# A fused attention and two-layer kernel: earlier weight stores, attention tile by tile, operands built in the last products

## The chip, the cores and the metric

The kernel runs on one core of a Trainium2 chip. The metric is the device time of one execution in microseconds, taken as the median of the runs shown. The core's engines work side by side, each through its own instructions in order: TensorE (PE in the profile, with PEld for its weight loads), VectorE (DVE), ScalarE (ACT), GpSimd (POOL) and SyncE (SP), which in this kernel issues every DMA.

## The reference, cut to what matters

```python
out[c] = softmax(scale * q_c @ [mem_k, k_ctx].T) @ [mem_v, v_ctx]      # chunks of 32 with local context
x  = heads of out side by side                                        # 3072 tokens x 512
x  = (sigmoid(x @ w_gate) * (x @ w_val)) @ w_out                       # 512 -> 1536 -> 512
h  = x @ w_in                                                         # 512 -> 2048
g  = (a0 + a1 h + a2 h^2 + a3 h^3) / (1 + |b0||h| + |b1| h^2 + 1e-6)
y  = g @ w_out                                                        # 2048 -> 512
```

All inputs and the result are float32. Each operand of a large product is split into a high and a low half (fp32r), and each product is three matmuls (high by high, high by low, low by high).

## The kernel before, in words

The 3072 tokens are 24 attention tiles of 128, and 6 blocks of 512. Attention of tiles 0 to 3 comes first (to about 31 us). Then 24 steps, numbered si, run the first layer on blocks 0 and 1 directly: step si is the slice f = si mod 12 of the 1536 hidden columns for block j = si // 12. A step is a gate product (`gate_val` with m = 0, 12 matmuls at L280), its sigmoid on ACT (L289), a value product (12 more at L280), the scaling on DVE (L292), the split of the result (`g_split`, L303 on ACT and L304 on DVE) and the out product of the step before (`out1`, L315).

A dictionary `plan`, filled by `at(si, function, arguments)`, says what else each step does. Within a step the order is written out: first the DMAs (loads of queries, keys, values, raw weights, and stores), then `w1_hi` (ACT, L263: high halves of the next step's three weights), `attn_exp` (ACT, L145), `bits1` (DVE, L236 and L243: the raw weights' bits), `s_add` (POOL, L367), then the gate product, `w1_lo` (DVE, L267: low halves), `attn_sum`, `attn_mul` (DVE), the attention products (L165 and L180), `s_split` (ACT L373, DVE L374), then the value product, and last `attn_qk` and `attn_max`. ACT changes its function table between exponential and sigmoid, which is an ACT_TABLE_LOAD each way.

Attention of tiles 4 to 15 lies in these steps. Tiles 8 to 15 are done in pairs: both tiles' exponentials stand in one step (12, 14, 16, 18). A tile at a sequence's edge (t mod 6 is 0 or 5) is copied by ACT (L117) and masked by a POOL memset (L119 or L122), and DVE takes its maximum behind that (L130); the others are read from PSUM (L137, L139).

The remaining blocks use seven products of halves in place of eight (`unit_s`, L436), for s = 1 and 2. Their weights need the raw gate and value weights in DRAM (`store_raw`, L351, tensor wsd) and four sums of them for each pair of slices: `s_add(p)` makes the sums on POOL from the raw weights of slices 2p and 2p+1, `s_split(p)` splits them into X and queues their store. The out weights go to DRAM too (L352, tensor wod). Their token operands come from xd: `load_b` loads four tiles (L383), and `build` makes differences (DVE L394) and splits them into X (ACT L390, DVE L391). X holds 14 slices; `SST` lists those for the sums' splits, `XS` those for the operands. At the end of step 23 the kernel issues `load_b(1)`, the first weights (`load_a`) and `build(1)`, ahead of the last two out products.

All big tiles come from one pool of 32 buffers (`wpool`): raw weights, split weights, queries, keys, values, sums and loaded operands. A tile taken from it waits for whatever last used that buffer, a store's landing among it. Work tiles of 2 KB a partition come from `tpool` (11), PSUM has four buffers `ps`, and a gate product's buffer comes free with its sigmoid. SP issues in order, and a DMA waits there for the landing of the DMA eight places before it.

The second layer runs from about 723 us. Its weights' splits are placed by `weights2`.

Of the kernel before, what the change touches and what calls it, by code (L numbers as in the profile page):

```python
# [8 lines left out]
F32 = mybir.dt.float32  # L9
# [12 lines left out]
P = 128  # L22
# [19 lines left out]
def fused_kernel(ctx: ExitStack, tc: tile.TileContext, q, k, v, w1, w2, coef, x2d, w2d, xd, gd, wsd, wod, out):  # L42
# [21 lines left out]
    cab = const.tile([P, 2], F32, name="cab")  # L64
    qc = const.tile([P, 1], F32, name="qc")
    nc.gpsimd.memset(qc, QC)

# [128 lines left out]
    def flush():  # L198
        for out_, in_ in pending:
            nc.sync.dma_start(out=out_, in_=in_)  # L200
        pending.clear()
# [137 lines left out]

    IDX = dict(A11=0, S2=1, S1=2, S3=3, A12=4, S4=5, A22=6)  # L340
    XS = (0, 2, 8, 10, 12, 4, 6)
    SST = (0, 1, 2, 3)

    def store_raw(f):

        p, odd = divmod(f, 2)
        for m in range(2):
            w = wp[1, 1, f, m].rearrange("p b (h k) -> p b h k", h=2)
            for name, h in ((("A22", 1),) if odd else (("A11", 0), ("A12", 1))):
                dst = wsd[p, :, m, IDX[name]].rearrange("p (b k) -> p b k", b=2)  # L350
                nc.sync.dma_start(out=dst, in_=w[:, :, h].bitcast(F32))  # L351
        nc.sync.dma_start(out=wod[f], in_=wp[1, 1, f, 2].bitcast(F32))  # L352

    ssum = {}
# [14 lines left out]

    def s_split(p):  # L370
        for i, (n, t) in enumerate(ssum.pop(p).items()):
            u = X[:, SST[i]].rearrange("p m (b k) -> p m b k", b=2)
            nc.scalar.activation(out=u[:, :, 0], in_=t, func=ACTF.Copy)  # L373
            nc.vector.tensor_tensor(out=u[:, :, 1], in0=t, in1=u[:, :, 0].bitcast(F32), op=ALU.subtract)  # L374
            pending.append((wsd[p, :, :, IDX[n]], X[:, SST[i]].bitcast(F32)))

    braw = {}

# [6 lines left out]
    def build(s):  # L385


        def split(i, t):
            hi, lo = (X[:, XS[i] : XS[i] + 2, b] for b in range(2))
            nc.scalar.activation(out=hi, in_=t, func=ACTF.Copy)  # L390
            nc.vector.tensor_tensor(out=lo, in0=t, in1=hi.bitcast(F32), op=ALU.subtract)  # L391

        def sub(out_, a, b):
            nc.vector.tensor_tensor(out=out_, in0=a, in1=b, op=ALU.subtract)  # L394

        b11, b12, b21, b22 = braw[0, 0], braw[0, 1], braw[1, 0], braw[1, 1]
        braw.clear()
        u1, u2 = (wpool.tile([P, 2, 512], F32, tag="w", name=f"bt{s}_{i}") for i in range(2))
        sub(u1, b12, b11)
        split(0, b11)  # L400
        sub(u2, b22, u1)
        split(1, u2)
        split(2, u1)
        sub(b12, b22, b12)
        split(3, b12)
        sub(u2, b21, u2)

        return [lambda: split(4, b21), lambda: split(5, b22), lambda: split(6, u2)]

    ast, wo = {}, {}  # L410

# [221 lines left out]
    def at(si, *call):  # L633
        plan.setdefault(si, []).append(call)
# [10 lines left out]
            if f > 2:  # L645
                at(max(si - 3, 0), load_w1, f)

    for t in range(4, 16, 2):
        s0 = (2, 5, 10, 12, 14, 16)[t // 2 - 2]
        for o, u in ((0, t), (1, t + 1)):  # L650
            at(s0 + o - 2, load_qk, u)
            at(s0 + o, attn_qk, u)
            at(s0 + o, attn_max, u)
            if t < 8:
                at(s0 + 3, attn_exp, u)
                at(s0 + o + 3, load_v, u)
                at(s0 + o + 3, attn_sum, u)
                at(s0 + o + 3, attn_mul, u)
                at(s0 + o + 4, attn_t, u)
                at(s0 + o + 5, pv, u)  # L660
            else:
                at(s0 + 2, attn_exp, u)
                at(s0 + o + 1, load_v, u)
                at(s0 + 2, attn_sum, u)
                at(s0 + 2, attn_mul, u)
                at(s0 + 3, attn_t, u)
                at(s0 + 4, attn_raw, u)

    for p, si in enumerate((11, 13, 15, 16, 18, 20)):
        at(si, s_add, p)  # L670
        at(si + 1, s_split, p)
    for f in range(NF1):
        at(NF1 + f, store_raw, f)
    w2_next = 0

    def weights2(k, n):
# [53 lines left out]
    with tc.manual_schedule():  # L730
# [69 lines left out]
        for si, (j, f, c0, n) in enumerate(steps):  # L800
            acts = plan.get(si, [])

            def run(*fns):
                for fn, *args in acts:
                    if fn in fns:
                        fn(*args)

            flush()
            run(load_qk, load_v, load_w1, store_raw)
            run(w1_hi, attn_exp, bits1, s_add)  # L810
            gate_val(j, f, 0, c0, n)
            run(w1_lo, attn_sum, attn_mul, pv, attn_raw, attn_t, s_split)
            gate_val(j, f, 1, c0, n)
            run(scale1)
            g_split((1, j, f, c0), sgs.pop((j, f, c0)), n)
            run(attn_qk, attn_max)
            if si == len(steps) - 1:
                flush()
                load_b(1)
                load_a(1, 0, 0)  # L820
                load_a(1, 0, 1)
                rest = build(1)
            if si:
                out1(*steps[si - 1])
        out1(*steps[-1])
        n_point = 0
        for s in range(1, NB // 2):
            for p in range(NP1 + 1):
                for m in range(2):
                    if p < NP1:  # L830
                        if m == 0:
                            load_wo(s, 0, 2 * p)
                        else:
                            load_wo(s, 0, 2 * p + 1)
                        if p == NP1 - 1:
                            load_wo(s, 1, m)
                            load_g(s, m)
                        unit_s(s, p, m, rest)
                        rest = []
                        load_a(s, p + 1, m)  # L840
                        point(n_point, s, 2 * (p - 1) + m if p else -1)
                        n_point += 1
                    else:
                        flush()
                        if m == 0:
                            load_g(s, 2)
                            load_wo(s, 1, 2)
                            if s == 1:
                                load_b(2)
                        out_s(s, 0, NF1 - 2 + m)  # L850
                        if m == 0:
                            g_split((1, 2 * s + 1, 0, 0), gb.pop(0), 512)
            for f in range(NF1):
                last = s == NB // 2 - 1
                load_wo(s, 1, f + 3)
                load_g(s, f + 3)
                if f + 1 < NF1:
                    g_split((1, 2 * s + 1, f + 1, 0), gb.pop(f + 1), 512)
                if last:
                    if f == 0:  # L860
                        nc.scalar.activation(out=cab, in_=cf[:, 4:6], func=ACTF.Abs)
                    if f >= NF1 - PRE:
                        h2(0, f - NF1 + PRE)
                if not last or f < NF1 - 1:
                    out_s(s, 1, f)
                if last:
                    if f % 2 == 0 and f < 2 * KT:
                        load_x2(0, f // 2)
                    if f % 2 == 1 and f < 2 * KT:
                        split_x2(0, f // 2)  # L870
                    if f == NF1 - 1:
                        for i in range(PRE - 1):
                            recip2(0, i)
                            ratio2(0, i)
                        split2(0, 0)
                    w2_next = weights2(w2_next, 2)
                elif f == 4:
                    load_a(2, 0, 0)
                    load_a(2, 0, 1)
                    rest = build(2)  # L880
        steps2 = [(j, f) for j in range(NB) for f in range(NF2)]
        for si in range(PRE, len(steps2) + LAG2):
            if si < len(steps2):
                j, f = steps2[si]
                if j == 0:
                    w2_next = weights2(w2_next, 1 if f > PRE + 1 else 0)
                if j + 1 < NB:
                    if f % 3 == 0 and 0 < f <= 3 * KT:
                        load_x2(j + 1, f // 3 - 1)
                    if f % 3 == 2 and 3 < f < 3 * KT + 3:  # L890
                        split_x2(j + 1, f // 3 - 1)
                h2(j, f)
                if si == PRE:
                    out_s(NB // 2 - 1, 1, NF1 - 1)
            if si >= LAG2:
                out2(*steps2[si - LAG2])
            if si - 1 < len(steps2):
                recip2(*steps2[si - 1])
                ratio2(*steps2[si - 1])
            if si - 2 < len(steps2):  # L900
                split2(*steps2[si - 2])
# [75 lines left out]
```

## Time and profile before

| | us |
|---|---|
| median of 3 runs | 1261.28 (1261.0 to 1262.39) |
| the profiled execution | 1263.89 |
| its span | 1262.0 |
| PE busy | 1173.4 (93%) |
| DVE busy | 951.7 (75%) |
| ACT busy | 717.9 (57%) |
| POOL busy | 37.1 (3%) |

The span is the time from the profile's first instruction to its last; 1.9 us of the execution lie around it. PE is busy for 93% of the span, but the share is an average over parts with different limits: cut into 40 slices of 31.5 us, PE is busy for six tenths of the time from 158 to 221 us, and the DMA engines for three tenths from 95 to 158 us. The rows below show these places.

### The profile page before, as it was taken

The page shows a single profiled execution, that of the slowest core. Times are in us where ns is not written, and L with a number is a line of the kernel's source. Part 1 is how long each engine was busy: PE and PEld are TensorE (multiplying, and loading weights), DVE is VectorE, ACT ScalarE, POOL GpSimd, SP SyncE. Part 2 cuts the span into 40 slices and gives each one's busy share as a digit, 9 for nine tenths or more (in the row PEclk, how much of TensorE's full clock was granted, in tenths as well). Part 3 has the DMA queues.
Part 4 walks back from the last instruction along what each step waited for, and adds up shares of the span by engine and source line. Part 5 has one row for each costly group of instructions (what it writes and reads, how often), then busy time and mean ns, then how long its engine had stood idle before and what let it go on. Part 6 is the DMA issues. An engine that isn't in the chain of part 4 may idle for free.

```text
span 1262.0 us, 20397 instructions
## 1 busy us (share of the span) xinstructions
PE 1173.4 (93%) x7920; PEld 952.0 (75%) x7920; DVE 951.7 (75%) x1496; ACT 717.9 (57%) x1222; POOL 37.1 (3%) x39
## 2 busy tenths in 40 slices
PE   4999966998999997899999899999999999999998
PEld 3787745786777776678888678788888888888887
DVE  6887546955766664467776579999888888898886
ACT  5876245653344341243333478886676677776765
POOL 0000103400000000000000000000000000000000
PEclk8999987999999999899999999999999999999999
DMA  9763358879988866779986932010010010100000
GB/s 369 275 200 114 121 199 288 295 251 328 358 313 320 320 244 237 288 271 358 355 327 216 381 126 59 26 51 17 9 51 9 9 50 9 50 17 1 34 1 34
DMA packets 95280, 220.22 MB, mean 175 GB/s; under 512 B 9168, under 2 KB 26576, under 8 KB 95184
## 3 DMA queue, kind: packets, MB, share of 16 engines
q1 hardware_dynamic: 95184, 218.93, 48.6%
q8 instruction: 62, 1.02, 0.3%
q14 instruction: 34, 0.28, 0.1%
HBM read 159.12 MB, written 59.77 MB: 173 GB/s over the span
## 4 chain that ended last, share of the span: by engine, by line
PE 47%; DVE 5%; DMA 2%; ACT 1%; issue 1%; SPq 0%; DVEq 0%; ACTq 0%
PE acc L577 19%; PE h L538 18%; PE u L436 7%; PE acc L490 3%; DMA w2f<-w2d 2%; DVE t L565 1%; DVE X L304 1%; DVE qq L564 1%; DVE wp L267 0%; DVE qq L551 0%; DVE t L550 0%; DVE t L549 0%; DMA wo<-wod 0%; DVE c L460 0%; DMA x2d<-x2s 0%
## 5 line engine op out<-in xcount | busy, mean ns | idle before, releaser
L538 PE MATMUL h<-X,wp 128*128 128x512 f32 x1152 | 276.7, 389 | 2.4 <-DVE wp L267 2.4
L577 PE MATMUL acc<-wp,X 128*128 128x512 f32 x1152 | 276.6, 389 | 1.0 <-ACT x2s L331 1.0
L538 PEld LDWEIGHTS h<-X,wp 128*128 128x128 f32 x1152 | 216.1, 188 | 47.7 <-DVE wp L267 2.8
L577 PEld LDWEIGHTS acc<-wp,X 128*128 128x128 f32 x1152 | 216.0, 188 | 46.8 <-ACT x2s L331 1.6
L436 PE MATMUL u<-X,a 128*128 128x512 f32 x1008 | 237.7, 393 | 11.1 <-DVE X L391 3.3
L436 PEld LDWEIGHTS u<-X,a 128*128 128x128 f32 x1008 | 188.8, 189 | 56.8 <-DVE c L460 5.0
L490 PE MATMUL acc<-g,wo 128*128 128x512 f32 x576 | 146.8, 404 | 17.6 <-ACT g L303 14.0
L280 PE MATMUL h<-X,wp 128*128 128x512 f32 x576 | 147.8, 410 | 9.7 <-ACT sg L289 6.2
L546 ACT ACTIVATE t<-h,cf 128x512 f32<-128x512 f32 x96 | 74.7, 778 | 123.1 <-PE h L538 119.9
L490 PEld LDWEIGHTS acc<-g,wo 128*128 128x128 f32 x576 | 109.1, 193 | 45.5 <-ACT g L303 16.3
L280 PEld LDWEIGHTS h<-X,wp 128*128 128x128 f32 x576 | 112.4, 198 | 36.0 <-ACT sg L289 6.9
L460 DVE TENSOR_TENSOR c<-c,u 128x512 f32<-128x512 f32 x168 | 111.5, 684 | 23.5 <-PE u L436 21.0
L549 DVE TENSOR_TENSOR t<-t,h 128x512 f32<-128x512 f32 x96 | 65.8, 686 | 40.5 <-ACT hh L548 39.0
L303 ACT ACTIVATE g<-sg 128x512 fp32r<-128x512 f32 x24 | 15.2, 632 | 121.5 <-DVE sg L453 121.5
L550 DVE SCALAR_TENSOR_TENSOR t<-t,cf,h 128x512 f32<-128x512 f32 x96 | 71.8, 748 | 3.4
L564 DVE SCALAR_TENSOR_TENSOR qq<-qq,y 128x512 f32<-128x512 f32 x96 | 65.8, 686 | 9.1 <-ACT y L559 9.1
L558 ACT ACTIVATE y<-qq,qc 128x512 f32<-128x512 f32 x96 | 69.9, 728 | 3.6 <-DVE qq L551 3.2
L551 DVE SCALAR_TENSOR_TENSOR qq<-hh,cab,qq 128x512 f32<-128x512 f32 x96 | 71.7, 747 | 0.0
L565 DVE SCALAR_TENSOR_TENSOR t<-t,cf,y 128x512 f32<-128x512 f32 x96 | 71.6, 746 | 0.0
L315 PE MATMUL acc<-X,wp 128*128 128x512 f32 x288 | 71.0, 396 | 0.0
L566 DVE SCALAR_TENSOR_TENSOR t<-qq,t 128x512 f32<-128x512 f32 x96 | 66.5, 693 | 3.3
L547 ACT ACTIVATE qq<-h,cab 128x512 f32<-128x512 f32 x96 | 65.4, 681 | 3.3 <-DVE t L565 3.3
(82 smaller groups left out, 1263.6 us busy)
## 6 DMA issues: line engine op xcount, KB each, us to landing
a<-wsd SPq DMA_DIRECT2D x72, 512.0 KB, 8.9
st<-w_in SPq DMA_DIRECT2D x68, 512.0 KB, 6.4
wo<-wod SPq DMA_DIRECT2D x48, 512.0 KB, 7.2
v<-v_in SPq DMA_DIRECT2D x24, 512.0 KB, 6.8
wsd<-X SPq DMA_DIRECT2D x24, 512.0 KB, 4.4
k<-k_in SPq DMA_DIRECT2D x24, 416.0 KB, 5.5
wsd<-wp SPq DMA_DIRECT2D x36, 256.0 KB, 5.2
w2d<-c SPq DMA_DIRECT2D x32, 256.0 KB, 4.1
```

What stands on the lines that cost most here:

```text
L280: nc.tensor.matmul(pt, lhsT=w[:, a, kt * P : (kt + 1) * P], rhs=x[:, kt, b, c0 : c0 + n], start=(kt == 0 and i == 0), stop=(kt == KT - 1 a ...
L315: nc.tensor.matmul(acc[j][d][:, c0 : c0 + n], lhsT=w[:, a, d * P : (d + 1) * P], rhs=g[:, b, 0:n], start=(f == 0 and c0 == 0 and i == 0), ...
L436: nc.tensor.matmul(bank, lhsT=w[:, a * 256 + kt * P : a * 256 + kt * P + P], rhs=X[:, XS[i] + kt, b], start=(kt == 0 and n == 0), stop=(kt ...
L460: nc.vector.tensor_tensor(out=out_, in0=a, in1=b, op=ALU.add)
L490: nc.tensor.matmul(acc[j][d], lhsT=w[:, a, d * P : (d + 1) * P], rhs=g[:, b], start=(f == 0 and i == 0), stop=(f == NF1 - 1 and i == 2),)
L538: nc.tensor.matmul(hp, lhsT=w[:, a, kt * P : (kt + 1) * P], rhs=x[:, kt, b], start=(kt == 0 and i == 0), stop=(kt == KT - 1 and i == 2),)
L546: nc.scalar.activation(out=t, in_=hp, func=ACTF.Identity, scale=cf[:, 3:4], bias=cf[:, 2:3])
L550: nc.vector.scalar_tensor_tensor(out=t, in0=t, scalar=cf[:, 1:2], in1=hp, op0=ALU.add, op1=ALU.mult)
L551: nc.vector.scalar_tensor_tensor(out=qq, in0=hh, scalar=cab[:, 1:2], in1=qq, op0=ALU.mult, op1=ALU.add)
L564: nc.vector.scalar_tensor_tensor(out=qq, in0=qq, scalar=QC, in1=y, op0=ALU.add, op1=ALU.mult)
L565: nc.vector.scalar_tensor_tensor(out=t, in0=t, scalar=cf[:, 0:1], in1=y, op0=ALU.add, op1=ALU.mult)
L577: nc.tensor.matmul(acc[j][m], lhsT=g[:, a, m * P : (m + 1) * P], rhs=w[:, b], start=(f == 0 and i == 0), stop=(f == NF2 - 1 and i == 2),)
```

## The change

The raw gate and value weights go to DRAM from the split weights of block 0 (steps 0 to 11) and not of block 1 (12 to 23); the out weights' store becomes `store_out` and stays in steps 12 to 23. Tiles 8 to 15 get a step each for every part of their attention. The sums' splits go round six slices of X, not four. `load_b(1)` moves to the start of step 22, `build(1)` is cut in two and its halves stand between the products of step 23 and ahead of `out1(22)`. `load_b(2)` moves behind the first out product of its block. The second layer calls `weights2` in two more of its steps, so its splits run two calls earlier. A tile of 32 bytes a partition stands before X.

```diff
+    const.tile([P, 8], F32, name="pad")
...
-    SST = (0, 1, 2, 3)
+    SST = (0, 1, 2, 3, 8, 9)
...
-            w = wp[1, 1, f, m].rearrange("p b (h k) -> p b h k", h=2)
+            w = wp[1, 0, f, m].rearrange("p b (h k) -> p b h k", h=2)
...
+    def store_out(f):
         nc.sync.dma_start(out=wod[f], in_=wp[1, 1, f, 2].bitcast(F32))
...
-            u = X[:, SST[i]].rearrange("p m (b k) -> p m b k", b=2)
+            u = X[:, SST[(4 * p + i) % 6]].rearrange("p m (b k) -> p m b k", b=2)
...
+        def first():
+            sub(u1, b12, b11)
+            split(0, b11)
+            sub(u2, b22, u1)
+            split(1, u2)
+        def second():
+            split(2, u1)
+            sub(b12, b22, b12)
+            split(3, b12)
+            sub(u2, b21, u2)
+        return [first, second, lambda: split(4, b21), lambda: split(5, b22), lambda: split(6, u2)]
...
-    for t in range(4, 16, 2):
-        s0 = (2, 5, 10, 12, 14, 16)[t // 2 - 2]
...
+    for u, s0 in zip(range(8, 16), (9, 10, 12, 13, 14, 16, 17, 18)):
+        at(s0 - 1, load_qk, u)
+        at(s0, attn_qk, u)
+        at(s0, attn_max, u)
+        at(s0 + 1, attn_exp, u)
+        at(s0 + 1, load_v, u)
+        at(s0 + 1, attn_sum, u)
+        at(s0 + 1, attn_mul, u)
+        at(s0 + 2, attn_t, u)
+        at(s0 + 3, attn_raw, u)
-    for p, si in enumerate((11, 13, 15, 16, 18, 20)):
+    for p, si in enumerate((11, 13, 15, 17, 18, 20)):
...
-        at(NF1 + f, store_raw, f)
+        at(f, store_raw, f)
+        at(NF1 + f, store_out, f)
...
+            if si == len(steps) - 2:
+                load_b(1)
-            run(load_qk, load_v, load_w1, store_raw)
+            run(load_qk, load_v, load_w1, store_raw, store_out)
             run(w1_hi, attn_exp, bits1, s_add)
             gate_val(j, f, 0, c0, n)
             run(w1_lo, attn_sum, attn_mul, pv, attn_raw, attn_t, s_split)
+            if si == len(steps) - 1:
+                load_a(1, 0, 0)
+                load_a(1, 0, 1)
+                rest = build(1)
+                rest.pop(0)()
             gate_val(j, f, 1, c0, n)
...
             if si == len(steps) - 1:
-                flush()
-                load_b(1)
-                load_a(1, 0, 0)
-                load_a(1, 0, 1)
-                rest = build(1)
+                rest.pop(0)()
...
-                            if s == 1:
-                                load_b(2)
...
+                elif f == 0:
+                    load_b(2)
...
-                    w2_next = weights2(w2_next, 1 if f > PRE + 1 else 0)
+                    w2_next = weights2(w2_next, 1)
```

On SP, at the end of the raw weights' loads (steps 7 to 9), only loads stood before; st_11 are raw weights of slice 11, and q, k and v are an attention tile's inputs:

```order
L222 DMA st_11_1_1355<-w_in 128x512
L222 DMA st_11_2_1357<-w_in 128x512
L89 DMA v_1359<-v_in 128x1024
L83 DMA q_1361<-q_in 128x512
L85 DMA k_1363<-k_in 128x832
L89 DMA v_1476<-v_in 128x1024
```

The same place now, where wp_0_7 are the split weights of step 7:

```order
L353 DMA wsd<-wp_0_7_0_1142 128x2x256
L353 DMA wsd<-wp_0_7_1_1144 128x2x256
L224 DMA st_11_0_1378<-w_in 128x512
L224 DMA st_11_1_1380<-w_in 128x512
L224 DMA st_11_2_1382<-w_in 128x512
L91 DMA v_1384<-v_in 128x1024
L85 DMA q_1386<-q_in 128x512
L87 DMA k_1388<-k_in 128x832
L353 DMA wsd<-wp_0_8_0_1268 128x2x256 x2
L353 DMA wsd<-wp_0_8_1_1270 128x2x256 x2
```

The stores of step 7's split weights stand ahead of the raw weights' loads, and those of step 8 ahead of the next tile's values.

On ACT, from the last high half of slice 11's weights (step 10), there stood before (sg are sigmoids, X<-sg the split of a scaled result, xp and tp attention products):

```order
L263 ACTIVATE wp_0_11_2_1561<-wfo_1374 128x512
L289 ACTIVATE sg_10_0_1576<-h_10_0_0_1563 128x512
L193 ACTIVATE X<-xp_0_1581 128x2x128
L193 ACTIVATE X<-xp_1_1582 128x2x128
L167 ACTIVATE at_1624<-tp_1619 128x512
L303 ACTIVATE X<-sg_10_0_1576 128x512
```

The same place now (line numbers are higher by 2; s is tile 8's scores):

```order
L265 ACTIVATE wp_0_11_2_1634<-wfo_1403 128x512
L147 ACT_TABLE_LOAD
L147 ACTIVATE s_1606<-s_1606 128x512
L291 ACT_TABLE_LOAD
L291 ACTIVATE sg_10_0_1650<-h_10_0_0_1637 128x512
L195 ACTIVATE X<-xp_0_1655 128x2x128
L195 ACTIVATE X<-xp_1_1656 128x2x128
L169 ACTIVATE at_1698<-tp_1693 128x512
L305 ACTIVATE X<-sg_10_0_1650 128x512
```

Tile 8's exponential with two table loads has come ahead of step 10's sigmoid; it stood with tile 9's in step 12.

On ACT, at the end of step 23 and the start of the seven-product part, there stood before (b and bt are the loaded token halves and their differences, x2s the finished block's result):

```order
L289 ACTIVATE sg_11_0_3267<-h_11_0_0_3254 128x512
L303 ACTIVATE X<-sg_11_0_3267 128x512
L390 ACTIVATE X<-b_00_3285 128x2x512
L390 ACTIVATE X<-bt_1_3310 128x2x512
L390 ACTIVATE X<-bt_0_3309 128x2x512
L390 ACTIVATE X<-b_01_3289 128x2x512
L331 ACTIVATE x2s_0_3347<-acc_0_2085 128x512
```

The same place now:

```order
L291 ACTIVATE sg_11_0_3276<-h_11_0_0_3263 128x512
L394 ACTIVATE X<-b_00_3201 128x2x512
L394 ACTIVATE X<-bt_1_3295 128x2x512
L305 ACTIVATE X<-sg_11_0_3276 128x512
L394 ACTIVATE X<-bt_0_3294 128x2x512
L394 ACTIVATE X<-b_01_3205 128x2x512
L333 ACTIVATE x2s_0_3348<-acc_0_2193 128x512
```

Two of the splits have moved ahead of the last split of a scaled result.

## Rows read from the trace of the kernel before

**Rows 1.** PE by line, 106.8 to 202 us: busy, mean | idle before <-releaser.
```profile
L280 PE MATMUL h<-X,wp 128*128 128x512 f32 x157 | 42.2, 420 | 7.4 <-ACT sg L289 6.2 <-DVE wp L267 1.2
...
L180 PE MATMUL xp<-at,v 64*64 64x32 f32 x320 | 6.6, 234 | 17.0 <-ACT sg L289 17.0
...
L165 PE MATMUL tp<-ident,s 128*128 128x128 f32 x16 | 2.5, 281 | 1.8 <-DVE s L139 1.8
```

**Rows 2.** The same, 202 to 302.3 us.
```profile
L280 PE MATMUL h<-X,wp 128*128 128x512 f32 x228 | 57.3, 403 | 1.0 <-issue 1.0
...
L180 PE MATMUL xp<-at,v 64*64 64x32 f32 x384 | 6.6, 220 | 0.6 <-ACT sg L289 0.6
...
L165 PE MATMUL tp<-ident,s 128*128 128x128 f32 x24 | 3.3, 273 | 0.8 <-DVE s L139 0.8
```

**Rows 3.** PE timeline: start us, us, instruction [idle before <-releaser].
```profile
116.24 2.89 PE L280 MATMUL h<-X,wp 128*128 128x512 f32 x12
...
133.00 4.61 PE L280 MATMUL h<-X,wp 128*128 128x512 f32 x12 [2.03 <-ACT sg L289]
...
165.22 4.35 PE L280 MATMUL h<-X,wp 128*128 128x512 f32 x12 [4.17 <-ACT sg L289]
...
199.93 1.93 PE L180 MATMUL xp<-at,v 64*64 64x32 f32 x62 [16.95 <-ACT sg L289]
201.79 4.83 PE L280 MATMUL h<-X,wp 128*128 128x512 f32 x12
```

**Rows 4.** POOL timeline, 165 to 200 us.
```profile
189.45 1.27 POOL L367 TENSOR_TENSOR S<-wfgv,wfgv 128x512 f32<-128x512 f32 x1 [17.54 <-issue]
...
191.99 0.15 POOL L122 MEMSET s<- 32x64 f32 x1
```

**Rows 5.** DMA issues, 181 to 191 us (median landing), and SP timeline.
```profile
wsd<-wp SPq DMA_DIRECT2D x2, 256.0 KB, 7.4
...
182.01 1.00 SPq L351 DMA_DIRECT2D wsd<-wp  x2
```

**Rows 6.** ACT timeline, 150 to 201 us.
```profile
158.71 0.63 ACT L263 ACTIVATE wp<-wfgv 128x512 fp32r<-128x512 f32 x1 [6.20 <-DMA wsd<-wp]
...
160.81 1.28 ACT L145 ACT_TABLE_LOAD   x1
162.11 1.15 ACT L145 ACTIVATE s<-s 128x512 f32<-128x512 f32 x2
...
194.88 0.63 ACT L263 ACTIVATE wp<-wfo 128x512 fp32r<-128x512 f32 x1 [15.12 <-DVE wp L267]
```

**Rows 7.** PE by line, then its timeline, 302.3 to 321 us.
```profile
L436 PE MATMUL u<-X,a 128*128 128x512 f32 x48 | 14.2, 444 | 4.8 <-DVE X L391 3.3 <-ACT X L390 1.1 <-DMA a<-wsd 0.4
...
306.05 2.79 PE L436 MATMUL u<-X,a 128*128 128x512 f32 x11 [0.76 <-DVE X L391]
...
314.20 7.13 PE L436 MATMUL u<-X,a 128*128 128x512 f32 x23 [1.80 <-DVE X L391]
```

**Rows 8.** Stretches: us, busy by engine, PE clock, DMA share, GB/s.
```profile
31.20:106.80 75.60, 73.27 (x605) 58.58 (x606) 66.94 (x117) 62.31 (x112) 0.34 (x2) 0.95 0.68 231
106.80:202.00 95.20, 69.00 (x822) 54.45 (x821) 50.84 (x95) 40.67 (x71) 10.71 (x9) 0.88 0.45 150
490.00:530.00 40.00, 27.41 (x100) 20.99 (x99) 16.61 (x19) 10.12 (x16) 0.00 (x0) 0.83 0.96 367
```

**Rows 9.** SP and ACT timelines, 45 to 76 us; the page's DMA issues.
```profile
53.93 1.40 SPq L222 DMA_DIRECT2D st<-w_in  x3
...
69.88 0.68 ACT L231 ACTIVATE st<-st 128x512 f32<-128x512 f32 x1
...
st<-w_in SPq DMA_DIRECT2D x68, 512.0 KB, 6.4
```

**Rows 10.** ACT timeline, 494 to 526 us.
```profile
504.64 0.63 ACT L303 ACTIVATE g<-gb 128x512 fp32r<-128x512 f32 x1 [12.10 <-DMA gb<-gd]
```

**Rows 11.** PE timeline, 734 to 900 us.
```profile
804.13 2.56 PE L538 MATMUL h<-X,wp 128*128 128x512 f32 x10 [2.42 <-DVE wp L267]
```

More of the change, by code (lines that the diff above doesn't have):

```diff
@@ L371, in s_split @@
         for i, (n, t) in enumerate(ssum.pop(p).items()):
-            u = X[:, SST[i]].rearrange("p m (b k) -> p m b k", b=2)
+            u = X[:, SST[(4 * p + i) % 6]].rearrange("p m (b k) -> p m b k", b=2)
             nc.scalar.activation(out=u[:, :, 0], in_=t, func=ACTF.Copy)
             nc.vector.tensor_tensor(out=u[:, :, 1], in0=t, in1=u[:, :, 0].bitcast(F32), op=ALU.subtract)
-            pending.append((wsd[p, :, :, IDX[n]], X[:, SST[i]].bitcast(F32)))
+            pending.append((wsd[p, :, :, IDX[n]], X[:, SST[(4 * p + i) % 6]].bitcast(F32)))
     braw = {}
@@ L398, in build @@
         u1, u2 = (wpool.tile([P, 2, 512], F32, tag="w", name=f"bt{s}_{i}") for i in range(2))
[L399 to L408, printed above, removed]
+        def first():
[9 more added lines that the diff above has]
+        return [first, second, lambda: split(4, b21), lambda: split(5, b22), lambda: split(6, u2)]
     ast, wo = {}, {}
@@ L646, in fused_kernel @@
                 at(max(si - 3, 0), load_w1, f)
-    for t in range(4, 16, 2):
-        s0 = (2, 5, 10, 12, 14, 16)[t // 2 - 2]
+    for t in range(4, 8, 2):
+        s0 = 2 if t == 4 else 5
         for o, u in ((0, t), (1, t + 1)):
@@ L653, in fused_kernel @@
             at(s0 + o, attn_max, u)
[L654 to L667, printed above, removed]
-    for p, si in enumerate((11, 13, 15, 16, 18, 20)):
+            at(s0 + 3, attn_exp, u)
+            at(s0 + o + 3, load_v, u)
+            at(s0 + o + 3, attn_sum, u)
+            at(s0 + o + 3, attn_mul, u)
+            at(s0 + o + 4, attn_t, u)
+            at(s0 + o + 5, pv, u)
+    for u, s0 in zip(range(8, 16), (9, 10, 12, 13, 14, 16, 17, 18)):
[9 more added lines that the diff above has]
+    for p, si in enumerate((11, 13, 15, 17, 18, 20)):
         at(si, s_add, p)
@@ L880, in fused_kernel @@
                     rest = build(2)
+                    rest.pop(0)()
+                    rest.pop(0)()
         steps2 = [(j, f) for j in range(NB) for f in range(NF2)]
```

## The prediction

> **What bounds the kernel now.** I read four views in this order. First the idle time of TensorE (PE) by line. It is the engine with the most work, and from 106.8 to 302.3 us it runs the last sixteen of the 24 steps of the direct part. The reader is to see that its idle time there lies in a few places: 7.4 us ahead of gate and value products, 17.0 ahead of attention products and 1.8 ahead of transposes up to 202 us [rows 1], and only 1.0, 0.6 and 0.8 us afterwards [rows 2]. That is 26.2 + 2.4 = 28.6 us in which PE has nothing to run.
>
> Second the PE timeline, which gives the places and their price in clock. The three long stalls end at 133.00, 165.22 and 199.93 us, and after each the next twelve products take 4.61, 4.35 and 4.83 us, where such a group takes 2.89 elsewhere [rows 3]. The difference, 1.7 + 1.5 + 1.9 = 5.1 us, is a granted clock at the lower level of 1.2 GHz in place of 2.4 GHz; it belongs to the stalls and goes with them. So 28.6 + 5.1 = 33.7 us hang on what stalls PE here.
>
> Third the chain behind the longest one, 16.95 us. GpSimd (POOL) starts the third sum of weight pair 1 at 189.45 after 17.54 us of idleness [rows 4]. The buffer that the sum takes was last that of the split weights of step 13, and their store was issued at 182.01 and took a median of 7.4 us to land, so about 189.4 [rows 5]. Behind the sum on POOL's queue is the mask of tile 11 (191.99) [rows 4]; VectorE (DVE) waits for it with the tile's maximum, the low halves of the next weights stand behind that on DVE, and ScalarE (ACT) waits 15.12 us for those until 194.88 [rows 6]. Exponentials and sigmoid come behind on ACT, and PE's next PSUM buffer comes free with the sigmoid. The 4.17 us stall at 165.22 has the same root: at 158.71 ACT had waited 6.20 us for a store of split weights to land, and then two table loads of 1.28 us and two exponentials (1.15 us) stood ahead of the sigmoid [rows 6].
>
> Fourth the start of the seven-product part: 4.8 us of idleness [rows 7], and 23 products in 7.13 us where eleven took 2.79, which would make 5.83: 1.3 us of clock [rows 7]. Together 6.1 us.
>
> **The change part by part.** *Stores from the first block.* The 36 stores of 256 KB keep their bytes, but are issued in steps 0 to 11, from the first block's split weights, not in 12 to 23. Only the stores of the third (out) weights stay there. In step 13 no sum's buffer then waits for a store of that step: the buffers that the sums of pair 1 and the weights of step 13 take were stored in steps 10 and 11, two steps and more earlier. The 16.95 and 4.17 us stalls and their clock (1.9 + 1.5) go. What is late next is the ordinary ACT and DVE queue.
>
> The price is in steps 0 to 8. They take 28 of the 36 stores: 28 x 256 KB = 7.3 MB in 75.6 us, 97 GB/s on top of 231; at 490 to 530 us the queues moved 367 GB/s at a share of 0.96 [rows 8]. 328 GB/s is thus about 0.86 of what they do: busy, not full. Each step's three weight loads are issued behind that step's stores. Their slack: the loads issued from 53.93 are first used at 69.88, and a load takes a median of 6.4 us to land, so 15.95 - 6.4 = 9.5 us are left [rows 9]. Bounds: 0, if the stores fit in that slack, and a stall as at 165.22 in each of the seven steps 4 to 10, 7 x (4.17 + 1.5) = 39.7 us. I take 1.5 us, near the lower end, because the share is below 1.
>
> *Attention tile by tile.* Tiles 8 to 15 get a step each: eight exponentials with two table loads each replace four pairs with two. That adds 8 loads x 1.28 = 10.3 us of ACT [rows 6]. ACT was busy for 40.67 of 95.2 us [rows 8], so in a steady step they lie beside PE's products. One place has no cover: in step 10 the sigmoid is already late (the stall at 133.00: 2.03 us, with 1.2 us for weights just ahead [rows 1, 3]), because DVE's bits of step 11's weights come late there, and the new exponential of tile 8 now stands ahead of that sigmoid: 2 x 1.28 + 0.6 = 3.2 us more. Bounds: nothing more, if DVE is the later of the two, and 3.2. I take all: 1.2 + 2.0 + 3.2 + 1.7 of clock = 8.1 us at this step, where 1.2 + 2.0 + 1.7 stood. Elsewhere I leave in the waits of an ordinary step: 1.8 us [rows 1] and 2.4 [rows 2], 4.2 in all; bounds 0 and the 22.4 of a rival below.
>
> The row shows a load of 1.28 us with the exponential at 162.11 right behind it, 0.02 us after its end [rows 6]. The Trainium skill, "ScalarE: Activation LUTs", section "What ACT_TABLE_LOAD costs", counts a drain of about 1.38 us beside each load, 2.66 us a switch, and its rule is to group functions by table set, which speaks against this change. By it the eight loads would be 21.3 us of ACT; the trace, in which no drain shows here, does not agree.
>
> *Token operands built in the last step.* The four token loads go to the start of step 22, the first splits between the two products of step 23, the next ahead of the last but one out product. Of the 6.1 us, the 0.4 us for the first weights' load stays [rows 7], and DVE and ACT now do the splits ahead of the last scaling of gate by value, which can hold the last out product back by some. Bounds: 0 and 6.1 left; I take 1.5: that 0.4 and the 1.1 us that now end on ACT's splits. Gain 4.6.
>
> *Ring of six and the tile of 32 bytes.* Two more slots for the sums' splits: the next pair does not wait for the store of the last. No row shows such a wait, so 0. The small tile moves addresses only: 0; I know no row that prices it, so a per cent of transfer time in either direction stays in the range.
>
> *Layer 1's third block.* The four token loads move behind the first out product of the second block. ACT's 12.10 us wait for its operand at 504.64 is one on transfers at a share of 0.96 [rows 8, 10], and the same transfers still precede the later operands: 0, bounds -2 and +2.
>
> *Layer 2.* Weight splits begin two calls earlier. The one wait, 2.42 us at 804.13, is PE waiting for such a split [rows 11]; two steps of head start cover it. Gain 2.4, bounds 0 and 2.4.
>
> *Sum.* 33.7 - 8.1 - 4.2 - 1.5 + 4.6 + 2.4 = 26.9 us. Against the profiled execution, 1263.9 us (span 1262.0 and 1.9 around it), that is 1237.0. The median of the runs is 2.6 us below the profiled one, so 1234.4; I say 1234.
>
> **The rivals.** *All exponentials on the path* (1256): the seven other tiles pay 3.2 us each as in step 10, 22.4 us. For it: ACT is in order and the sigmoid frees PE's buffer. Against it: from 202 us on, with pairs of exponentials in the queue too, PE waits for a sigmoid for 0.6 us in all [rows 2]. By the skill's drain on each load it would be 7 x 2 x 1.38 = 19 us more.
>
> *The hole only moves* (1253): some other buffer's store or load holds a sum or a mask in POOL's order, and the 17.0 us and 1.9 of clock come back at another tile. For it: POOL's order of sums and masks stays, and tiles 11 and 12 still have masks beside sums. Against it: no store of the big weights is left in steps 12 to 23.
>
> *Early stores starve the first block, slower* (1272): stores ahead of the loads on the one queue, in order, push each step's weights back by more than 9.5 us; from that point ACT waits and each of steps 4 to 10 stalls by 4.17 + 1.5 us: 39.7 less the 1.5 in the sum is 38 more than the forecast. For it: the share rises from 0.68 to some 0.86. Against it: the slack of 9.5 us, and the loads run four steps ahead.
>
> *Nothing new stalls* (1219): the 12.3 us of steps 9 to 23 and the 1.5 do not appear, and only some of the transition: 15 us better.
>
> **How the numbers follow.** Forecast 0.60 (1225 to 1245), exponentials 0.10, moved hole 0.10, starved block 0.08, nothing new 0.12. A range of 1218 to 1258 leaves out the starved block and some of the moved hole above, and little below: 0.17. Within 0.2% (2.5 us) is what cannot be told from no change; the starved block in part, or two of the rivals at once, would give it, 0.04. Slower 0.10, faster 0.86.
>
> **What would show it.** On PE no stall above 6 us between 106.8 us and the end of the direct part, and that end near 282 us in place of 302 (33.7 - 8.1 - 4.2 - 1.5 = 19.9 earlier); about 5 us at step 10, with ACT's exponential ahead of the sigmoid; POOL's third sum of pair 1 without a wait. In steps 1 to 8 steps of 8 to 10 us as before; if they are longer, with ACT waiting for loads, the sum is wrong there. The first seven-product units should start with under 2 us of waits, and no wait of 2.4 us should stand in layer 2. What would make the prediction wrong: sigmoids late in most steps from 13 on, or a new stall of over 10 us that ends on a store.

## The result

The changed kernel takes 1233.66 us (median; 1233.05 to 1235.02) against 1261.84 of the kernel before: ratio 0.9776, 95% interval 0.9759 to 0.9793, so 26 to 30 us less. The forecast was 1234. Its profiled execution took 1233.17 us with a span of 1231.4, 30.6 below the span before; the sum in the prediction, made against the same profiled execution, said 26.9. The time came out, in part by luck, as the last sections show: most terms of the sum were off by 1 to 2 us, and the cause that was named for the largest is one of two. One execution of the run old_build, of 1936.5 us, lies far from its other three and is left out of what follows.

Idle time of PE by line in the changed kernel, 106.8 to 202 us, which answers to [rows 1] (the changed kernel's line numbers are higher by 2 here and by 8 further down; the columns are the same):

```profile
L282 PE MATMUL h<-X,wp 128*128 128x512 f32 x208 | 53.3, 405 | 2.3 <-ACT sg L291 2.1 <-DVE wp L269 0.2
...
L182 PE MATMUL xp<-at,v 64*64 64x32 f32 x448 | 8.6, 225 | 3.2 <-DVE s L141 2.2 <-DVE sg L294 1.0
L167 PE MATMUL tp<-ident,s 128*128 128x128 f32 x28 | 4.9, 303 | 0.0
```

26.2 us have become 5.5, and PE does more in the same stretch: 208 matmuls of gate and value products for 157. The PE timeline of the changed kernel shows where the rest is; it answers to [rows 3]:

```profile
114.72 2.88 PE L282 MATMUL h<-X,wp 128*128 128x512 f32 x12
...
125.21 2.59 PE L282 MATMUL h<-X,wp 128*128 128x512 f32 x10 [0.20 <-DVE wp L269]
128.78 0.30 PE L182 MATMUL xp<-at,v 64*64 64x32 f32 x2 [0.98 <-DVE sg L294]
131.25 1.51 PE L182 MATMUL xp<-at,v 64*64 64x32 f32 x62 [2.18 <-DVE s L141]
132.69 1.11 PE L167 MATMUL tp<-ident,s 128*128 128x128 f32 x4
134.85 4.77 PE L282 MATMUL h<-X,wp 128*128 128x512 f32 x12 [1.04 <-ACT sg L291]
...
189.88 3.01 PE L282 MATMUL h<-X,wp 128*128 128x512 f32 x12 [1.04 <-ACT sg L291]
...
232.25 3.01 PE L282 MATMUL h<-X,wp 128*128 128x512 f32 x12 [1.10 <-ACT sg L291]
```

Step 10 is the one place with a price: 0.20 + 0.98 + 2.18 + 1.04 = 4.4 us of waits, and at the lower clock 1.9 us more in the value product, 0.4 and 0.45 more in the attention products before it. From there to step 23 two waits of 1.04 and 1.10 us are all that PE has. On POOL the third sum of pair 1 (164.41) now follows the second without a wait, as the timeline shows, in place of [rows 4]:

```profile
162.77 1.68 POOL L371 TENSOR_TENSOR S<-S,wfgv 128x512 f32<-128x512 f32 x1
164.41 1.30 POOL L371 TENSOR_TENSOR S<-wfgv,wfgv 128x512 f32<-128x512 f32 x1
```

The stretches of [rows 8] in the changed kernel:

```profile
31.20:106.80 75.60, 73.61 (x611) 59.10 (x612) 66.91 (x117) 62.40 (x114) 0.34 (x2) 1.00 0.91 320
106.80:202.00 95.20, 89.62 (x1100) 71.40 (x1100) 69.54 (x116) 61.87 (x105) 23.31 (x18) 0.96 0.57 199
```

The DMA share of the first rose from 0.68 to 0.91 and the rate from 231 to 320 GB/s (the prediction had worked out 0.86 and 328), and PE lost nothing by it: steps 2 to 7 start within 0.12 us of before, and step 9 at 114.72 against 116.24. The run late_stores below, the same kernel without these stores, takes 66.8 us from step 2 to step 9 (47.43 to 114.22), and so does the changed kernel (47.95 to 114.72).

The end of step 23 and the start of the seven-product part, on PE; it answers to [rows 7]:

```profile
270.72 2.88 PE L317 MATMUL acc<-X,wp 128*128 128x512 f32 x12
275.86 0.50 PE L317 MATMUL acc<-X,wp 128*128 128x512 f32 x1 [2.25 <-ACT X L305]
276.58 2.83 PE L317 MATMUL acc<-X,wp 128*128 128x512 f32 x11 [0.22 <-DVE X L306]
279.25 8.98 PE L444 MATMUL u<-X,a 128*128 128x512 f32 x36
289.19 11.13 PE L444 MATMUL u<-X,a 128*128 128x512 f32 x48 [0.95 <-issue]
```

The first 36 products of halves run without a wait; 2.25 and 0.22 us stand ahead of the last out product instead, and 0.95 us behind the 36. In layer 2 the waits ahead of L546 (L538 before) are 0.1 us in all:

```profile
L546 PE MATMUL h<-X,wp 128*128 128x512 f32 x1152 | 276.7, 389 | 0.1
```

Between points that both PE timelines show, the 30.6 us lie like this (before, after, gained, and what the sum in the prediction had):

| stretch of PE's timeline | before | after | gained | forecast |
|---|---|---|---|---|
| start to step 9's gate product (116.24; 114.72) | 116.2 | 114.7 | 1.5 | -1.5 |
| to step 23's gate product (291.28; 265.28) | 175.0 | 150.6 | 24.5 | 21.4 |
| to a wait of 0.68 us on DVE's c in the next part (330.95; 301.78) | 39.7 | 36.5 | 3.2 | 4.6 |
| to a wait of 0.21 us on issue at the third part (548.92; 518.91) | 218.0 | 217.1 | 0.8 | 0 |
| to the out products before layer 2 (717.31; 688.18) | 168.4 | 169.3 | -0.9 | 0 |
| to the end (1262.0; 1231.4) | 544.7 | 543.2 | 1.5 | 2.4 |

### The profile page after: what moved, and what is told of

Same layout as the page of the kernel before. It is cut to its first block, busy times and chain, and to the rows that moved or that the text cites. A ratio compares the mean times of both kernels' runs of the same rounds, so it can differ in the third digit from the quotient of the medians.

```text
span 1231.4 us, 20428 instructions
## 1 busy us (share of the span) xinstructions
PE 1174.2 (95%) x7920; PEld 954.3 (77%) x7920; DVE 952.2 (77%) x1496; ACT 727.4 (59%) x1230; POOL 36.9 (3%) x39
## 4 chain that ended last, share of the span: by engine, by line
PE 48%; DVE 5%; DMA 2%; ACT 1%; issue 1%; DVEq 0%; ACTq 0%; SPq 0%
PE acc L585 19%; PE h L546 18%; PE u L444 7%; PE acc L498 3%; DMA w2f<-w2d 2%; DVE t L558 1%; DVE X L306 1%; DVE t L573 1%; DVE wp L269 1%; DVE qq L572 1%; DVE qq L559 1%; DMA x2d<-x2s 1%; DVE t L557 1%; DVE c L468 0%; ACT wp L265 0%
## 5 line engine op out<-in xcount | busy, mean ns | idle before, releaser
L546 PE MATMUL h<-X,wp 128*128 128x512 f32 x1152 | 276.7, 389 | 0.1
L546 PEld LDWEIGHTS h<-X,wp 128*128 128x128 f32 x1152 | 216.3, 188 | 45.2 <-DVE X L529 0.5
L498 PE MATMUL acc<-g,wo 128*128 128x512 f32 x576 | 149.4, 410 | 13.8 <-ACT g L305 10.8
```

The costliest lines, as they stand in the source:

```text
L498: nc.tensor.matmul(acc[j][d], lhsT=w[:, a, d * P : (d + 1) * P], rhs=g[:, b], start=(f == 0 and i == 0), stop=(f == NF1 - 1 and i == 2),)
L546: nc.tensor.matmul(hp, lhsT=w[:, a, kt * P : (kt + 1) * P], rhs=x[:, kt, b], start=(kt == 0 and i == 0), stop=(kt == KT - 1 and i == 2),)
```

## The experiments

Theory A is the prediction's: the early stores take away the waits that made the two long stalls. Theory B: attention tile by tile does. Theory C came after the first four runs: the long stall, the hole, needs both a store that is late and its buffer handed to a sum. Ratios are to the kernel before in the same session; the changed kernel's is 0.9776.

**Late stores in the changed kernel** (late_stores).

```diff
-            w = wp[1, 0, f, m].rearrange(...)
+            w = wp[1, 1, f, m].rearrange(...)
-        at(f, store_raw, f)
+        at(NF1 + f, store_raw, f)
```

> The changed kernel with one part undone: gate and value weights are stored in steps 12 to 23 from the second block's split weights again. Theory A (the stores' landing is what held buffers, and so caused the stalls of 4.17 and 16.95 us with some 4 us of clock): most of about 25 us comes back, 1252 to 1259 us, with ACT or POOL waiting for a store of split weights. Theory B (attention tile by tile removed the stalls, since one exponential and one mask stand where two stood): within 5 us of the changed kernel, 1233 to 1239 us.

Measured: 1231.95 us, ratio 0.9748 (0.9732 to 0.9765). Theory A falls as the only account: nothing came back. On POOL, late_stores shows the third sum of pair 1 without a wait, although the stores of steps 12 and 13 are late again. The first two rows are POOL's timeline, the last is SP's; this store, of step 13's weights, is issued 9 us behind the sum:

```profile
162.15 1.68 POOL L371 TENSOR_TENSOR S<-S,wfgv 128x512 f32<-128x512 f32 x1
163.78 1.29 POOL L371 TENSOR_TENSOR S<-wfgv,wfgv 128x512 f32<-128x512 f32 x1
...
173.06 1.64 SPq L353 DMA_DIRECT2D wsd<-wp  x2
```

The sum's buffer can no longer be that of step 13's weights, since it is written before their store is even issued: with tiles taken from the pool of 32 in another order, the buffers fall otherwise. By the compiled program the keys of tile 10 lay in it before; no row of the trace shows that.

**Early stores alone in the kernel before** (early_only).

```diff
-            w = wp[1, 1, f, m].rearrange(...)
+            w = wp[1, 0, f, m].rearrange(...)
+    def store_out(f):
-        at(NF1 + f, store_raw, f)
+        at(f, store_raw, f)
+        at(NF1 + f, store_out, f)
-            run(load_qk, load_v, load_w1, store_raw)
+            run(load_qk, load_v, load_w1, store_raw, store_out)
```

> The kernel before with the early stores alone (pairs of tiles, the old place of the operands' build, the old ring, the old layer 2). Theory A: 1262 - 25 = about 1237 us, no stall above 5 us left between 106 and 302 us, stall at step 10 as before (1.2 + 2.0 us and its clock). Theory B: the stalls shrink but stay, 1248 to 1258 us.

Measured: 1247.51 us, ratio 0.9881 (0.9855 to 0.9908): 12 to 18 us faster, not 25. By its time it lies at the edge of theory B's range and 10 us above theory A's. The PE timeline of early_only, from an execution of 1253.69 us (the other three took 1246.75 to 1248.14):

```profile
165.05 0.66 PE L165 MATMUL tp<-ident,s 128*128 128x128 f32 x4 [1.23 <-DVE sg L292]
...
168.56 1.09 PE L165 MATMUL tp<-ident,s 128*128 128x128 f32 x4 [2.85 <-DVE s L139]
...
184.89 1.92 PE L180 MATMUL xp<-at,v 64*64 64x32 f32 x62 [2.67 <-ACT sg L289]
...
233.07 1.13 PE L180 MATMUL xp<-at,v 64*64 64x32 f32 x62 [1.76 <-ACT sg L289]
```

No stall above 5 us is left, as A had it, and up to the end of the direct part no instruction waits for such a store. But steps with two tiles still stall by 1.2 to 2.9 us. Two tiles' exponentials and maxima in one step thus seem to have a price of their own, which the hole had covered; the next run bears on it.

**Pairs of tiles in the changed kernel** (pairs).

```diff
-    for u, s0 in zip(range(8, 16), (9, 10, 12, 13, 14, 16, 17, 18)):
...
+    for t in range(4, 16, 2):
+        s0 = (2, 5, 10, 12, 14, 16)[t // 2 - 2]
...
-    for p, si in enumerate((11, 13, 15, 17, 18, 20)):
+    for p, si in enumerate((11, 13, 15, 16, 18, 20)):
```

> The changed kernel with attention of tiles 8 to 15 in pairs again and the sums of pair 3 in step 16. Theory A: tile by tile is worth little by itself, 1231 to 1237 us; step 10 loses its exponential and gets some 2 us shorter, and steps with two exponentials may wait 1 to 3 us for a sigmoid. Theory B: 1245 us or more.

Measured: 1238.91 us, ratio 0.9802 (0.9787 to 0.9816). Between the two: beside the early stores tile by tile is worth about 3 us by the ratios (their intervals overlap) and 5 by the profiled spans (1236.5 and 1231.4). In steps 9 to 22 themselves it is 8.4 us (158.9 against 150.6); the rest of the trace gives 3 us back, in places that the edit does not touch. The four stalls just shown stand in pairs too (1.22, 2.85, 2.67 and 1.76 us). The prediction had tile by tile as a cost of 3.2 us.

**Both back** (late_pairs): pairs, with the edit of late_stores.

> The changed kernel with the late stores and the pairs of tiles both back, so without the two parts of which either alone had removed the hole of 16.95 us. Theory C (the hole needs both: a sum whose buffer was last that of step 13's weights, which pairs of tiles give, and a store of those weights that is issued late): the hole of about 17 us and the stall of about 4 us come back with their clock, 1252 to 1258 us. Rival (one of the other parts, ring, build or layer 2, removed it in the run with late stores): 1231 to 1240 us.

Measured: 1255.6 us, ratio 0.9945 (0.9926 to 0.9965), as theory C has it. PE's, POOL's and SP's timelines of late_pairs:

```profile
163.89 4.98 PE L282 MATMUL h<-X,wp 128*128 128x512 f32 x12 [5.36 <-ACT sg L291]
...
197.20 1.93 PE L182 MATMUL xp<-at,v 64*64 64x32 f32 x62 [15.56 <-ACT sg L291]
...
186.72 1.26 POOL L371 TENSOR_TENSOR S<-wfgv,wfgv 128x512 f32<-128x512 f32 x1 [16.13 <-issue]
...
179.37 1.47 SPq L353 DMA_DIRECT2D wsd<-wp  x2
```

The first of these two stores landed at 186.59, and the sum started at 186.72. In the kernel before, the store issued at 182.01 landed at 189.33, and the sum started at 189.45: what the prediction had worked out from a median holds for the store itself.

So, with all else as in the changed kernel: both parts 1233.7, tiles alone 1232.0, stores alone 1238.9, neither 1255.6 us. Either part removes the hole; they do not add. Beside tile by tile, the early stores are worth nothing that these times show.

**Sums' buffers taken first, in the kernel before** (sums_first).

```diff
-            run(load_qk, load_v, load_w1, store_raw)
-            run(w1_hi, attn_exp, bits1, s_add)
+            run(s_add)
+            run(load_qk, load_v, load_w1, store_raw)
+            run(w1_hi, attn_exp, bits1)
```

> The kernel before, where each step takes its sums' buffers before its loads' and its weights' buffers; stores, attention and everything else as before. The third sum of pair 1 then gets a buffer of step 12's weights, whose store is issued a step earlier. Theory C: the hole of 16.95 us shrinks to 0 to 3 us, the 4.17 us stall at step 12 stays, since its buffer is the same; some 15 to 19 us faster than before. Rival (the order of masks and sums on GpSimd and the pair of exponentials make the hole, whatever the buffer): 0 to 4 us faster.

Measured: 1261.87 us, ratio 0.9998 (0.9978 to 1.0018): the time is a miss, since 15 to 19 us were expected. The hole at its place is gone: 2.61 us stand where 16.95 stood, with stores and attention as before. But other buffers have changed with it. PE's timeline of sums_first, then ACT's:

```profile
185.78 1.46 PE L180 MATMUL xp<-at,v 64*64 64x32 f32 x62 [2.61 <-ACT sg L289]
...
217.05 1.93 PE L180 MATMUL xp<-at,v 64*64 64x32 f32 x62 [7.96 <-ACT sg L289]
...
198.11 1.15 ACT L263 ACTIVATE wp<-wfgv 128x512 fp32r<-128x512 f32 x2 [4.76 <-DMA wsd<-wp]
...
210.96 1.15 ACT L263 ACTIVATE wp<-wfgv 128x512 fp32r<-128x512 f32 x2 [6.43 <-DMA wsd<-wp]
```

ACT's high halves have got buffers whose stores are not yet landed, 4.76 and 6.43 us, and a new hole of 7.96 us follows. Step 14 is 15.4 us shorter than before, but steps 13, 16 and 18 are 17.8 us longer. This is the prediction's rival of the moved hole, in this kernel and not in the changed one.

**Stores ahead of a step's other DMAs, in the kernel before** (store_first); the buffers stay.

```diff
+            run(store_raw)
             flush()
-            run(load_qk, load_v, load_w1, store_raw)
+            run(load_qk, load_v, load_w1)
```

> The kernel before, where each step issues its weights' stores ahead of its other DMAs (sums' splits, loads); the buffers are the same. The store of step 13's weights then stands behind the block's result stores (to 175.3 us) but ahead of the sums' splits and three loads, so it is issued about 6.7 us earlier than at 182.01. Theory C: the hole shrinks by 5 to 7 us to 10 to 12 us, 4 to 8 us faster than before. Rival (the transfer itself is late whatever its place, since the DMA engines are full): less than 2 us.

Measured: 1251.11 us, ratio 0.9907 (0.9882 to 0.9932): 9 to 15 us, more than expected. SP's and PE's timelines of store_first:

```profile
171.97 0.97 SPq L351 DMA_DIRECT2D wsd<-wp  x2
...
161.55 3.06 PE L280 MATMUL h<-X,wp 128*128 128x512 f32 x12 [0.41 <-ACT sg L289]
...
185.68 1.93 PE L180 MATMUL xp<-at,v 64*64 64x32 f32 x62 [5.13 <-ACT sg L289]
```

The store is issued at 171.97 in place of 182.01, and the hole is 5.13 us in place of 16.95; at 165.22 the 4.17 us went too (0.41), since the store of step 12 moved as well, which the expectation had missed. With the order of buffers and the attention untouched, moving the stores up the queue takes most of the hole away.

**The small parts, each undone in the changed kernel** (old_build, no_w2, old_b2).

```diff
-            if si == len(steps) - 2:            # old_build
-                load_b(1)
...
+                flush()
+                load_b(1)
+                load_a(1, 0, 0)
+                load_a(1, 0, 1)
+                rest = build(1)
+                rest.pop(0)()
                 rest.pop(0)()
```

```diff
-                    w2_next = weights2(w2_next, 1)            # no_w2
+                    w2_next = weights2(w2_next, 1 if f > PRE + 1 else 0)
```

```diff
+                            if s == 1:            # old_b2
+                                load_b(2)
...
-                elif f == 0:
-                    load_b(2)
```

> The changed kernel with the token loads and the operands' build of the next part back at the end of step 23. My account: the waits of 4.8 us and 1.3 us of clock at the start of the seven-product part come back and the 2.5 us ahead of the last out product go: 3.6 us slower than the changed kernel, 1236 to 1239 us. Rival: the loads are hidden anyway, and it makes less than 1 us.

> The changed kernel with layer 2's weight splits two calls later again. My account: PE waits 2.4 us for one split at the end of block 0 of layer 2, 2 to 3 us slower than the changed kernel, about 1236 us. Rival: the wait was an accident of the earlier parts and stays away, 1233 to 1234 us.

> The changed kernel with the four token loads of the third part back ahead of the second block's out products. My account: the same transfers on full queues, so only the places of the waits at 470 to 500 us move: 0, within 2 us of the changed kernel. Rival: the move took the first operands ahead of those loads and is worth the 2 to 3 us by which the waits there shrank in sum, 1235 to 1237 us.

Measured: 1234.19 us (0.9767, 0.9746 to 0.9788), 1233.0 (0.9761, 0.9747 to 0.9776) and 1232.11 (0.9755, 0.9740 to 0.9770). None differs from the changed kernel by what the times can tell, so the expected 3.6 and 2.4 us fail as times. Their traces show the mechanisms in place all the same. PE's timeline of old_build, and the one wait of layer 2 in no_w2:

```profile
280.17 2.83 PE L444 MATMUL u<-X,a 128*128 128x512 f32 x11 [0.76 <-DVE X L395]
283.59 0.49 PE L444 MATMUL u<-X,a 128*128 128x512 f32 x1 [0.58 <-ACT X L394]
284.85 1.68 PE L444 MATMUL u<-X,a 128*128 128x512 f32 x6 [0.77 <-DVE X L395]
288.31 3.17 PE L444 MATMUL u<-X,a 128*128 128x512 f32 x11 [1.78 <-DVE X L395]
```

```profile
773.42 2.57 PE L546 MATMUL h<-X,wp 128*128 128x512 f32 x10 [2.40 <-DVE wp L269]
```

From step 23's gate product to the same wait on c in the next part, old_build takes 38.5 us (266.52 to 305.02) against 36.5: the part saves 2.0 us there. From the out products before layer 2 (686.75) to the end, no_w2 takes 544.5 against 543.2: 1.2 us. Differences of that size, one way and the other, lie elsewhere in each trace and cover them.

The small parts can also be read together: late_pairs differs from the kernel before by them alone (the ring and the small tile with them), and it is 4 to 9 us faster, where the prediction had 4.6 + 2.4 = 7.0. Its trace has 2.9 us of that from step 23 to the wait on c and 1.5 in layer 2; the rest lies in no one place.

**Tiles 8 and 9 a step later** (tile8_later), a variant of the changed kernel.

```diff
-    for u, s0 in zip(range(8, 16), (9, 10, 12, 13, 14, 16, 17, 18)):
+    for u, s0 in zip(range(8, 16), (10, 11, 12, 13, 14, 16, 17, 18)):
```

> The changed kernel with tiles 8 and 9 one step later each (scores in steps 10 and 11, exponentials in 11 and 12). Theory A: the four waits of step 10 (0.2, 1.0, 2.2, 1.0 us) with 2.7 us of clock shrink to those of the kernel before or less: 2 to 4 us faster than the changed kernel, 1230 to 1232 us. Rival: the late bits of slice 11's weights on DVE alone cause them, so they stay: 1233 to 1235 us.

Measured: 1230.23 us, ratio 0.9726 (0.9706 to 0.9746), in the expected range. Step 10's four waits are gone; 0.69 us at 158.14 and 1.89 at 161.74 are new. Step 10 takes 10.87 us, where the changed kernel takes 18.83 and the kernel before 16.28. The run does not tell the exponential from the other cause that the prediction named, the late bits of slice 11's weights on DVE: they start at 116.63 us here without a wait, but at 120.86 in the changed kernel and at 122.37 in the kernel before, in both behind a wait for a gate or value product.

**Eight steps running, and earlier token loads** (best).

```diff
-    for u, s0 in zip(range(8, 16), (9, 10, 12, 13, 14, 16, 17, 18)):
+    for u, s0 in zip(range(8, 16), (10, 11, 12, 13, 14, 15, 16, 17)):
-            if si == len(steps) - 2:
+            if si == len(steps) - 3:
```

> The changed kernel with tiles 8 to 15 in eight steps running (scores in steps 10 to 17), and the next part's token loads at the start of step 21, one step earlier. Expected: the stalls of step 10 shrink as in the run with tiles 8 and 9 later, and the 2.25 us ahead of the last out product, which ended on ACT and DVE building operands whose loads came late, goes: 1226 to 1230 us. Rival: three steps in a row with exponentials in steps 14 to 17 make sigmoids late, and nothing is won over 1230 us.

Measured: 1230.4 us, ratio 0.9749 (0.9729 to 0.9769): the rival's value. Its mechanism shows in part: PE waits 0.46, 1.10 and 0.47 us at 206.55, 209.36 and 222.38, where tile8_later has one wait of 1.11. And the 2.25 us stayed to the hundredth. ACT's timeline of best, then DVE's, show why:

```profile
266.51 0.60 ACT L291 ACTIVATE sg<-h 128x512 f32<-128x512 f32 x1 [4.01 <-PE h L282]
267.01 1.05 ACT L394 ACTIVATE X<-b 128x1024 fp32r<-128x1024 f32 x1
...
263.14 1.22 DVE L398 TENSOR_TENSOR bt<-b,b 128x1024 f32<-128x1024 f32 x1
268.09 1.23 DVE L395 TENSOR_TENSOR X<-b,X 128x1024 fp32r<-128x1024 f32 x1 [3.73 <-ACT X L394]
...
271.63 1.23 DVE L395 TENSOR_TENSOR X<-bt,X 128x1024 fp32r<-128x1024 f32 x1 [1.18 <-ACT X L394]
272.77 0.68 DVE L294 TENSOR_TENSOR sg<-sg,h 128x512 f32<-128x512 f32 x1
```

The loads had landed: DVE's first difference ran at 263.14. But ACT's first split stands behind step 23's sigmoid, which waits for the gate product, and DVE's scaling at 272.77 stands behind DVE's half of the splits.

**The first half of the build ahead of the gate product** (best2).

```diff
             run(w1_hi, attn_exp, bits1, s_add)
+            if si == len(steps) - 1:
+                rest = build(1)
+                rest.pop(0)()
             gate_val(j, f, 0, c0, n)
...
-                rest = build(1)
-                rest.pop(0)()
```

> As the run named best, with the first half of the operands' build ahead of the gate product of step 23 in place of behind it. In best the token loads had landed, but ACT's first split still stood behind step 23's sigmoid, and DVE's scaling of gate by value behind DVE's half of those splits, so 2.25 us and some 1.8 us of clock stayed ahead of the last out product. Expected: they go, 3 to 4 us faster than best, 1226 to 1228 us. Rival: the build holds step 23's sigmoid, and nothing is won: 1229 to 1231 us.

Measured: 1226.31 us, ratio 0.9709 (0.9693 to 0.9725), as expected; the lowest median of all, though its interval overlaps that of tile8_later. PE's timeline of best2 runs through:

```profile
267.49 5.60 PE L317 MATMUL acc<-X,wp 128*128 128x512 f32 x24
272.93 8.62 PE L444 MATMUL u<-X,a 128*128 128x512 f32 x36
```

From step 23's gate product to the wait on c it takes 33.05 us (262.05 to 295.10), against 36.5 in the changed kernel and in best. The ring of six and the small tile were not tried alone.

## Why the prediction was right, and where its steps were not

**The stalls (33.7 us, the two long ones above all).** Right in size: 24.5 us gained in steps 9 to 22 is 33.7 less 7.1 at step 10 and 2.1 of two waits. The chain that it read (store, sum's buffer, mask, low halves, sigmoid) is shown by store_first, where only the place of the stores changed, and by late_pairs, where store and sum follow each other as in the kernel before. Wrong as the prediction put it was that the stores from the first block are what takes it away: late_stores has none of them and no hole. What the runs show in its place is that the hole needs a late store and a buffer handed to a POOL sum too early, and each of the two large parts takes one of them away. That tile by tile does so is luck: it changed the order in which buffers are taken, and where they would fall was no part of the plan. In sums_first another order took the hole away and made a new one.

**Step 10 (8.1 us).** 7.1: 4.4 of waits and 2.7 of clock. The added exponential stands ahead of the sigmoid as foreseen (table load at 130.96, sigmoid at 134.20 in ACT's timeline), but only 1.04 us of the waits end on that sigmoid; 3.4 us end on DVE before it. tile8_later removes all of it, the waits that stood there before included, so the term could have been nothing.

**Ordinary waits (4.2).** 2.1. The pairs made more of them than a single tile does: "attention tile by tile" was mis-sized with the wrong sign. It cost 2.1 us at step 10 (7.1, where 5.0 stood) and took away the waits of the pairs' steps: as a whole it is worth 3 to 5 us of the time beside the early stores. The eight added table loads cost PE little after step 10: both waits left end on a sigmoid that stands behind one exponential and its two loads (185.99 to 189.23 and 228.37 to 231.60 us in ACT's timeline), 2.1 us where the rival of all exponentials on the path had 22.4.

**Early stores' price (1.5).** None, at a DMA share of 0.91: the same steps take 66.8 us with and without them. The slack of 9.5 us held.

**Operands (4.6).** 3.2, in part because 2.25 + 0.22 us moved ahead of the last out product, which the step had named as a risk and taken as 1.1 us. best and best2 show its cause: the order on ACT and DVE, not the loads.

**Layer 2 (2.4).** The wait is gone, 1.2 to 1.5 us of it remain as a gain.

By the table the sum was 3.0 us short at the start (1.5 of price and 1.5 of clock, below), 3.1 short in the steps, and 2.3 long in operands and layer 2; 3.7 us short of the profiled gain in all, and 1.3 short of the medians, which are 28.2 us apart. That 1234 meets the median within 0.4 us is luck. The sum gave 1237.0 for a profiled execution that took 1233.17; the 2.6 us that the forecast then took off, because the median had been that much below the profiled execution, did not come back: the changed kernel's median lies 0.5 us above its own. The two errors, 3.8 and 3.1 us, nearly cancel.

## What to carry to other kernels

Where buffers of one pool serve loads, weights and sums, a wait on a store belongs to a pair: a buffer that comes round, and a store that is late. Look for both before naming the cause, since undoing either alone may change nothing. Work put ahead of a needed instruction on an in-order engine is only early if what stands ahead of it there is not waiting: read which instruction it stands behind, not only whether its data have landed.

## What was not expected of the hardware

A stall of the same size was followed by the lower of the two clock levels in one execution and not in another: after 1.50 us ahead of attention products at 98.15, the kernel before ran its next value product in 4.59 us (99.62); after 1.63 us at 98.22, the changed kernel ran it in 3.02. The 1.5 us are in the first line of the table above. They are no work of the edit: old_build has the changed kernel's instructions up to there and takes 4.32 us. Step 7, which holds these products, takes 13.25 to 13.44 us in five of the fourteen traces and 11.71 to 11.81 in the other nine. The first two rows are the changed kernel's, the next two those of the kernel before, the last two those of old_build:

```profile
98.22 1.13 PE L182 MATMUL xp<-at,v 64*64 64x32 f32 x62 [1.63 <-DVE s L141]
...
99.69 3.02 PE L282 MATMUL h<-X,wp 128*128 128x512 f32 x12
...
98.15 1.13 PE L180 MATMUL xp<-at,v 64*64 64x32 f32 x62 [1.50 <-DVE s L139]
...
99.62 4.59 PE L280 MATMUL h<-X,wp 128*128 128x512 f32 x12
...
97.93 1.13 PE L182 MATMUL xp<-at,v 64*64 64x32 f32 x62 [1.61 <-DVE s L141]
...
99.68 4.32 PE L282 MATMUL h<-X,wp 128*128 128x512 f32 x12
```

Nor was it expected that a DMA share of 0.91, with 28 stores more by the end of this stretch, would delay no step.
